# Opening order, first loads and one closing unit in a fused attention and mixer kernel on one Trainium2 core

## The chip, the cores and the metric

The kernel runs on one core of one Trainium2 chip. The core has engines that run side by side, each with its own instruction queue in order: TensorE (PE in the profile, its weight loads PEld), VectorE (DVE), ScalarE (ACT), GpSimd (POOL), and SyncE (SP), whose queue here issues the DMAs. The metric is the device time of one execution in microseconds (us), lower is better. Three runs of the kernel before gave 985.40, 985.25 and 983.98 us, median 985.25.

## What is computed

Inputs are float32: `z` (8, 3136, 64), `v` and `u` (8, 3136, 256), and the mixer's weights `U` (3136, 32), `V` (32, 3136), `w_ch1` (256, 1024) and `w_ch2` (1024, 256).

```python
scores = np.matmul(z, z.transpose(0, 2, 1)) / S        # S = 3136
attn = np.maximum(scores, 0.0) ** 2
x = u * np.matmul(attn, v)                             # attention part
h = (x.transpose(0, 2, 1) @ U) @ V                     # mixes along the sequence
u2 = x + h.transpose(0, 2, 1)
out = u2 + np.maximum(u2 @ w_ch1, 0.0) @ w_ch2
```

The score matrix of a batch is symmetric, since both factors are `z`.

## The kernel before

**Tiles and slots.** The 3136 rows of a batch are 24 tiles of 128 rows (`NF`) and a tail of 64. Four tiles make a group of 512 rows, so a batch has six full groups (`NQ`) and a small one; `NG` is 7. One (batch, group) is an item, and the main loop has one slot for each of the 56 items. In a slot TensorE does three kinds of work, cut into short units that are interleaved: the attention-by-`v` matmuls of this item (`av_stream`), the score matmuls that later items need (`todo[t]`), and the mixer matmuls of an item seven or eight slots back (`u2_unit`, `ch1_part`, `ch2_stream`). After the last slot a closing loop of `NQ + 1` stages (L1466 on) does the mixer of the last batch.

**Score pairs.** A score pair is two matmuls of 64 x 128 by 64 x 512 into the two banks of one PSUM buffer, one on the upper 64 rows of TensorE's array and one on the lower (`score_pairs`, L424; every paired matmul is recorded as `pair`'s line L182). The result goes through a scale and ReLU (`rectify`, on ScalarE at L386 or on VectorE at L382 and L393) and a square (L362 on VectorE; one early pair entirely on ScalarE, L376 and L377), and lands as bf16 in one of 20 score blocks (`take_block`). From the second batch on, and in late groups of the first, half of the score blocks come from the other half by a DMA transpose (L416 for 512 columns, L408 for pieces). For the first groups of batch 0 there is nothing to transpose from in time, and those are computed twice, so score pairs, ReLUs and squares are densest in slots 0 to 2.

**Who decides the order.** Instructions are in a manual schedule: what the Python code emits first on an engine stands first in its queue. Planner variables choose the order: `clock[0]` counts TensorE's work in units of one 256-column pair, `free_at` holds the expected times of ScalarE, VectorE and SP, `ps_free` the expected times at which the four PSUM buffers (two banks each) come free. `take_ps` takes the buffer that is expected free first, `rectify` gives work to the engine expected free first, and `hold(time, f)` puts off a DMA or a cast until the planner's clock has passed a time. These numbers set only the order; on the chip the engines wait for each other by semaphores.

**The opening.** `z` and `v` of batch 0 are loaded and cast, and `z` is turned (64 columns to partitions) by matmuls against an identity matrix, `ident`, in three turns (`z_turn`, L323: matmuls L329, copy out of PSUM L338): tiles 0 to 3, tiles 4 to 7, and an eight-tile turn of tiles 8 to 15. Two more turns (tiles 16 to 23, and the tail) follow inside slot 0, behind casts of L240. Blank matmuls of `ident` by `ident` run ahead of them: 18 at the start (L1285) and 10 ahead of the eight-tile turn (L327). They compute nothing that is used. `ident` is made by two POOL instructions. Two score pairs stand between the second and the eight-tile turn, two after it; then slot 0 starts.

**First loads.** The mixer's weights are needed only from slot 7 on. `first_loads` (L1217) says in which slot each begins: slot 1 and 2 `V` (16 DMAs of L1198, four casts into `V4_bf`), slot 3 `U` (L1156, L1157), slot 4 `w_ch1` (L1172), slot 5 `w_ch2` (L1175). All of them use SP's queue, which also carries the loads of `v` (L254), `u` (L306) and `z` (L218, L224) and the DMA transposes. The casts go to ScalarE (L202) or VectorE (L204), whichever the planner has free first, and are held back for some time after the slot's start.

**The closing loop.** For an item, `u2_unit` (L808) makes `h` in PSUM, adds `x` on VectorE (L855) and usually casts the sum and turns it by DMA (L770) for the next matmul. For the item called `direct`, the last batch's first group, the turned form is made another way (`u2T_unit`), and its `u2_unit(..., turn=False)` yields only the sum that is added to the output. In `qm.append((17, 1, False, f))` the first number is the place in the stage, counted in units of `ch2_stream`, at which `f` is emitted. Around it stand ReLUs of the first mixer layer (L944 on VectorE, L947 on ScalarE) and the output adds (L1067).

The functions that the diff touches:

Of the kernel before, what the change touches and what calls it, by code (L numbers as in the profile page):

```python
# [9 lines left out]
BF16 = mybir.dt.bfloat16  # L10
# [8 lines left out]
def kernel(  # L19
# [11 lines left out]
    nc = tc.nc  # L31

    B, S, D = u.shape
# [3 lines left out]
    P = 128  # L37
# [6 lines left out]
    GT = 4  # L44
# [10 lines left out]
    NG = len(groups)  # L55
# [6 lines left out]
    persist = ctx.enter_context(tc.tile_pool(name="persist", bufs=1))  # L62
# [3 lines left out]
    ctx.enter_context(tc.manual_schedule())  # L66

    ident = persist.tile([P, P], BF16, name="ident")
    w1_bf = persist.tile([P, ND, H], BF16, name="w1_bf")
    w2_bf = persist.tile([P, NH, D], BF16, name="w2_bf")  # L70
    U_bf = persist.tile([P, NT, R], BF16, name="U_bf")
# [5 lines left out]
    NQ = NF // GT  # L77
# [18 lines left out]
    clock = [0.0]  # L96
# [14 lines left out]
    def book(eng, ready, cost):  # L111
        free_at[eng] = max(free_at[eng], ready) + cost
        return free_at[eng]
# [5 lines left out]
    def hold(due, f):  # L119
        held.append((due, len(held), f))  # L120
# [18 lines left out]
    def pe(cost):  # L139
        clock[0] += cost  # L140
# [3 lines left out]
    ps_free = [0.0] * NPS  # L144

    def take_ps():
        k = min(range(NPS), key=lambda i: ps_free[i])
        assert ps_free[k] < float("inf")
        clock[0] = max(clock[0], ps_free[k])
        ps_free[k] = float("inf")  # L150
        for bank in range(2):
            wrote.pop((k, bank), None)
        return k, ps_pool.tile([P, 2, GW], FP32, name=f"ps{k}")
# [169 lines left out]
    def z_turn(b, t0, copy, n=2 * GT, warm=0):  # L323
        n = min(n, NT - t0)
        k, pz = take_ps()
        for _ in range(warm):
            nc.tensor.matmul(out=pz[:, 0, :P], lhsT=ident, rhs=ident, start=True, stop=True)  # L327
        for q in range(n):
            nc.tensor.matmul(  # L329
                out=pz[:, q // GT, (q % GT) * P : (q % GT + 1) * P],  # L330
                lhsT=z_bfs[b][:, t0 + q, :, :].rearrange("p c d -> p (c d)"),
                rhs=ident,
                start=(q % GT == 0),
                stop=(q % GT == GT - 1 or q == n - 1),
            )
        flat = pz.rearrange("p a c -> p (a c)")
        dst = zzTs[b].rearrange("p t c -> p (t c)")[:, t0 * P : (t0 + n) * P]
        copy(out=dst, in_=flat[:, : n * P])  # L338
        pe(8)
        ps_free[k] = book("act", clock[0] + 3, 9.5)  # L340


    def half(zzT, jj, c0, n):
# [800 lines left out]
    def jobs_of(b, g):  # L1144
        js = [J for J in range(NQ) if J >= g or made_twice(b, g, J)]
        j = [(b, g, (J, h)) for J in js for h in range(2)]
        if g % 2 == 0 and b == 0:
            j.append((b, g, "last"))
        return j
# [18 lines left out]
    def load_w(k):  # L1168
        def step(i):
            entry, raw = stage_block()  # L1170
            if k == 0:
                nc.sync.dma_start(out=raw, in_=moe_w_ch1[i * P : (i + 1) * P, :])  # L1172
                dst = w1_bf[:, i, :]
            else:
                nc.sync.dma_start(  # L1175
                    out=raw.rearrange("p (t d) -> p t d", d=D),
                    in_=moe_w_ch2.rearrange("(t p) d -> p t d", p=P)[:, i * GT : (i + 1) * GT, :],
                )
                dst = w2_bf[:, i * GT : (i + 1) * GT, :].rearrange("p t d -> p (t d)")
            queued(GT * D / 2)  # L1180

            def casts(entry=entry, raw=raw, dst=dst):
                cast(dst, raw, GT * D)
                give_block(entry)

            return [casts]

        return [lambda i=i: step(i) for i in range(2)]


    def load_V(i0):
        n = P // 4

        def step(i):
            entry, raw = stage_block()
            w = n * NF + (S - NF * P if i == 3 else 0)
            for c in range(NREP):
                nc.sync.dma_start(out=raw[c * R : (c + 1) * R, :w], in_=moe_V[:, i * n * NF : i * n * NF + w])  # L1198
                queued(w / 8)

            def casts(i=i, entry=entry, raw=raw):
                cast(
                    V4_bf[:, : NF * P].rearrange("r (t p) -> r t p", p=P)[:, :, i * n : (i + 1) * n],
                    raw[:, : n * NF].rearrange("r (p t) -> r t p", t=NF),
                    2 * n * NF,
                )
                if i == 3:
                    nc.vector.memset(V4_bf[:, S:], 0.0)
                    cast(V4_bf[:, NF * P : S], raw[:, n * NF : n * NF + S - NF * P], 100)
                give_block(entry)  # L1210

            return [casts]

        return [lambda i=i: step(i) for i in range(i0, i0 + 2)]


    first_loads = {  # L1217
        1: lambda: load_V(0),
        2: lambda: load_V(2),
        3: lambda: [load_U],  # L1220
        4: lambda: load_w(0),
        5: lambda: load_w(1),
    }


# [5 lines left out]
    on_act, on_dve, on_pool = nc.scalar.copy, nc.vector.tensor_copy, nc.gpsimd.tensor_copy  # L1231
# [49 lines left out]
    spare += [lambda i=i: cast_v(i, on_pool) for i in range(1, NQ)]  # L1281

    k, ps = take_ps()
    for _ in range(18):
        nc.tensor.matmul(out=ps[:, 0, :P], lhsT=ident, rhs=ident, start=True, stop=True)  # L1285
    ps_free[k] = 36
    cast_z(0, 0, on_dve, 0, GT)
    cast_z(0, 1, on_act, 0, GT)
# [1 line left out]
        cast_z(0, c, on_dve, GT, 2 * GT)  # L1290
    for i in range(2):
        give_block(zraw[i][2])
    clock[0] = 38
    z_turn(0, 0, on_act, GT)
    z_turn(0, GT, on_act, GT)
    clock[0] = 43
    free_at.update(dve=46, act=47)
    jobs0 = jobs_of(0, 0)
    score_burst(jobs0[:1])
    score_burst(jobs0[1:2])  # L1300
    clock[0] = 56
    z_turn(0, 2 * GT, on_act, warm=10)
    score_burst(jobs0[2:3])
    score_burst(jobs0[3:4])
    clock[0] = 72

    todo = {t: [] for t in range(n_items)}
    for b in range(B):
        for g in range(NQ):
            t = b * NG + g - 1  # L1310
            new = jobs_of(b, g)
            if g == 0 and b > 0:
                x, y = (5, 10) if b == 1 else (5, 11)
                todo[t - 2] += new[:x]
                todo[t - 1] += new[x:y]
                todo[t] += new[y:12] if b == 1 else new[y:]
                todo[t + 1] += new[12:] if b == 1 else []
            elif b == 0 and g == 0:
                todo[0] += new[4:]
            elif b == 0 and g and g % 2 == 0:  # L1320
                todo[t] += new[:-1]
                todo[t + 1] += new[-1:]
            else:
                todo[t] += new

    for t, most in ((0, 15), (1, 16), (2, 13)):
        todo[t + 1] = todo[t][most:] + todo[t + 1]
        todo[t] = todo[t][:most]

    direct = (B - 1, 0)  # L1330
# [4 lines left out]
    for t in range(n_items):  # L1335
# [6 lines left out]
        g_now = t % NG  # L1342
        b_next = t // NG + 1
# [6 lines left out]
            xTs[direct] = take_block()[1][:, : GT // 2, :].rearrange("p a (q d c) -> p (a q) d c", d=ND, c=P)  # L1350
            x_turn(*direct, xTs[direct])
        for i, f in enumerate(casts_next):
            hold(clock[0] + (90 if g_now == NQ and b_next > 1 else 15 if t >= NQ else 45) + 12 * i, f)
        casts_next = []
        spare += spare_next
        spare_next.clear()
# [26 lines left out]
        qc, qs, qm = [], [], []  # L1383
# [13 lines left out]
        if av and full:  # L1397
# [5 lines left out]
            n = len(mine) - 3  # L1403
            qs += [(9 + 74 * i / n, 1, False, lambda: scores(1)) for i in range(n)]
        elif av:
# [5 lines left out]
            k = min(2, len(mine) // 3)  # L1411
            n = len(mine) - 3 * k
            at = [1 + 80 * i / n for i in range(n)]
            if t == 0:
                at, k = [14, 30, 44, 50, 64, 68, 78, 84, 92], 0
# [46 lines left out]
    def small_parts(item, places):  # L1462
        box = {}
        return [(x, 1 - way, False, lambda way=way: ch1_small(*item, way, box)) for way, x in enumerate(places)]

    for k in range(NQ + 1):  # L1466
        fin = (B - 1, k - 1) if k else (B - 2, NQ - 1)
        mix = (B - 1, k) if k < NQ else None
        light = ch2_halves(*fin) if k == NQ else ch2_stream(*fin, {}).units
        first, qm = parts(mix, {}) if mix else [], []  # L1470
        if k == 0:
            qc = small_parts((B - 2, NQ), (13, 19)) + queue((16, 18, 20, 21, 24, 26, 28, 30), first)
            qm.append((3, 0, False, lambda: u2T_unit(*direct)))
            qm.append((9, 1, False, lambda: u2_unit(B - 1, 1)))
            qm.append((17, 1, False, lambda: u2_unit(*direct, turn=False)))
            qm.append((25, 1, False, lambda: u2_unit(B - 1, 2)))
        else:
            last = k == NQ - 1
            qc = queue((1, 2, 5, 6, 10, 11, 14, 16) if last else (1, 4, 8, 12, 16, 20, 24, 28), first)
            if k + 2 <= NQ:  # L1480
                qm.append((2, 1, False, lambda: u2_unit(B - 1, k + 2)))
            if last:
                qc += small_parts((B - 1, NQ), (18, 23))
            if k == 1 or k == NQ:
                qm.append((9, 1, False, lambda b=B - 2 if k == 1 else B - 1: ch2_small(b, NQ)))
        emit(light, [qc, qm])
# [30 lines left out]
```

## Time and profile before

The profiled execution took 985.75 us; its span in the trace is 984.0 us.

| what | number |
|---|---|
| median of three runs | 985.25 us |
| profiled execution / its span | 985.75 / 984.0 us |
| TensorE busy | 974.5 us (99%) |
| VectorE busy | 630.0 us (64%) |
| ScalarE busy | 484.3 us (49%) |
| POOL busy | 16.5 us (2%) |
| matmuls | 16165 |
| symmetric turns and other DMA transposes (blk from blk) | 156, 5.2 us each from issue to landing |
| weights `w_ch1`, `w_ch2` | 4 DMAs of 512 KB, 7.6 us each |

In a timeline line the numbers are start and length in us, then engine, line, operation, tiles (out, then in), the shape and the count of instructions taken together; square brackets hold the engine's idle time before the line and what ended it. The chain is followed back from the last instruction, and shows at each step what released it.

### The profile page before, as it was taken

Reading aid. Unit: us, or ns where it says so; the run is one execution under the profiler, and the core shown is the slowest. Engines: PE = TensorE matmul, PEld = TensorE weight load, DVE = VectorE, ACT = ScalarE, POOL = GpSimd, SP = SyncE. Lnnn points to the kernel's source line nnn. Section 1 sums busy time; section 2 is a strip of 40 time slices with the busy share of each in tenths; the row PEclk is TensorE's granted clock in tenths of the full one; section 3 lists DMA queues with packets and bytes.
Section 4 is the critical chain, followed back from the end, with each engine's and each line's share of the span. In section 5 each row is a group of like instructions: output and inputs, shape, how many; then the busy total and the mean of one; then the engine's idle time right before and its main releaser. Section 6 shows DMA issues by size and latency. Waiting matters only on the chain.

```text
span 984.0 us, 35373 instructions
## 1 busy us (share of the span) xinstructions
PE 974.5 (99%) x16165; PEld 778.2 (79%) x16165; DVE 630.0 (64%) x811; ACT 484.3 (49%) x560; POOL 16.5 (2%) x25
## 2 busy tenths in 40 slices
PE   9999999999999999999999999999999999999998
PEld 6788777877778777787777877788777887778766
DVE  7877855668556685567755667556775567653363
ACT  7887732456324463355533555334653345531353
POOL 4100000000000000000000000000000000000000
PEclk9999999999999999999999999999999999999999
DMA  9999999979997799987999779998799978975143
GB/s 266 201 237 205 219 191 187 220 152 186 203 207 158 174 184 188 213 167 180 182 203 207 146 178 191 212 198 147 173 211 202 194 148 165 177 136 103 46 113 99
DMA packets 372405, 176.37 MB, mean 179 GB/s; under 512 B 347296, under 2 KB 350624, under 8 KB 372256
## 3 DMA queue, kind: packets, MB, share of 16 engines
q1 hardware_dynamic: 372256, 174.12, 86.4%
q8 instruction: 126, 2.06, 0.9%
q14 instruction: 23, 0.19, 0.1%
HBM read 62.56 MB, written 25.69 MB: 90 GB/s over the span
## 4 chain that ended last, share of the span: by engine, by line
PE 94%; DVE 2%; ACT 2%; DMA 1%; SPq 0%; POOL 0%; issue 0%; DVEq 0%; POOLq 0%
PE ps L182 91%; DVE blk L362 1%; PE ps L701 1%; ACT blk L386 1%; PE ps L782 1%; DMA u2T<-x_bf 1%; DMA blk<-in_moe_V_dram 0%; PE ps L1081 0%; DVE blk L382 0%; PE ps L1285 0%; ACT blk L947 0%; PE ps L329 0%; POOL v_bf L1246 0%; PE ps L327 0%; SPq L1198 0%
## 5 line engine op out<-in xcount | busy, mean ns | idle before, releaser
L182 PEld LDWEIGHTS <-blk 64*128 64x128 bf16 x12288 | 613.8, 94 | 153.3 <-POOLq L172 9.5
L182 PE MATMUL ps<-v_bf,blk 64*128 64x256 bf16 x9216 | 611.7, 269 | 0.3
L386 ACT ACTIVATE blk<-ps 128x1024 bf16<-128x1024 f32 (+1 forms) x331 | 312.1, 971 | 343.8 <-PE ps L182 341.7
L362 DVE TENSOR_TENSOR blk<-blk 128x1024 bf16<-128x1024 bf16 x351 | 222.7, 659 | 46.6 <-ACT blk L386 45.9
L182 PE MATMUL ps<-u2T,w_bf 64*128 64x512 bf16 (+1 forms) x1792 | 227.7, 349 | 0.3 <-DMA u2T<-x_bf 0.2
L182 PE MATMUL ps<-w_bf,blk 64*128 64x256 bf16 x3072 | 192.4, 269 | 0.2 <-ACT blk L947 0.2
L944 DVE TENSOR_SCALAR blk<-ps 128x1024 bf16<-128x1024 f32 x106 | 129.7, 1224 | 93.3 <-PE ps L182 92.3
L947 ACT ACTIVATE blk<-ps 128x1024 bf16<-128x1024 f32 x86 | 87.3, 1022 | 117.8 <-PE ps L182 117.5
L182 PE MATMUL ps<-zzT 64*128 64x512 bf16 (+2 forms) x902 | 130.8, 328 | 2.2 <-ACT blk L386 1.5
L182 PEld LDWEIGHTS <-w_bf 64*128 64x128 bf16 x1792 | 84.4, 94 | 27.4 <-POOLq L172 5.0
L734 DVE TENSOR_TENSOR x_bf<-ps,u_sb 128x1024 bf16<-128x1024 f32 x48 | 58.7, 1222 | 72.8 <-PE ps L182 72.8
L855 DVE TENSOR_TENSOR out_sb<-ps,x_bf 128x1024 f32<-128x1024 f32 x42 | 51.4, 1223 | 59.1 <-PE ps L182 59.1
L1067 DVE TENSOR_TENSOR out_sb<-ps,out_sb 128x1024 f32<-128x1024 f32 x42 | 51.4, 1224 | 18.6 <-PE ps L182 18.3
L182 PEld LDWEIGHTS <-zzT 64*128 64x128 bf16 x902 | 41.7, 94 | 8.6 <-issue 3.9
L382 DVE TENSOR_SCALAR blk<-ps 128x1024 bf16<-128x1024 f32 (+1 forms) x17 | 19.6, 1159 | 7.1 <-PE ps L182 7.1
L182 PE MATMUL ps<-t_sb,V_bf 64*128 64x256 bf16 x200 | 20.6, 269 | 0.0
L202 ACT CAST v_bf<-stage 128x1024 bf16<-128x1024 f32 x18 | 18.7, 1042 | 0.0
L182 PE MATMUL ps<-v_bf,last_sb 64*128 64x256 bf16 x192 | 18.5, 269 | 0.2 <-POOLq L172 0.2
L204 DVE CAST v_bf<-stage 128x1024 bf16<-128x1024 f32 (+1 forms) x30 | 18.1, 603 | 0.0
L204 DVE CAST x_bf<-out_sb 128x1024 bf16<-128x1024 f32 x21 | 14.5, 688 | 0.3
L202 ACT CAST x_bf<-out_sb 128x1024 bf16<-128x1024 f32 x14 | 14.5, 1037 | 0.0
L362 DVE TENSOR_TENSOR attn_small<-attn_small 128x1600 bf16<-128x1600 bf16 x8 | 7.9, 990 | 9.0 <-ACT attn_small L591 9.0
(80 smaller groups left out, 241.1 us busy)
## 6 DMA issues: line engine op xcount, KB each, us to landing
u_sb<-in_u_dram SPq DMA_DIRECT2D x48, 512.0 KB, 5.0
stage<-in_v_dram SPq DMA_DIRECT2D x42, 512.0 KB, 6.1
out_dram<-out_sb SPq DMA_DIRECT2D x42, 512.0 KB, 3.1
stage<-in_z_dram SPq DMA_DIRECT2D x7, 512.0 KB, 5.9
blk<-in_v_dram SPq DMA_DIRECT2D x5, 512.0 KB, 6.3
out_dram<-blk SPq DMA_DIRECT2D x5, 512.0 KB, 2.6
blk<-blk SPq DMA_TRANSPOSE x156, 5.2
blk<-in_moe_w_ch_dram SPq DMA_DIRECT2D x4, 512.0 KB, 7.6
```

The lines of the kernel that those rows point to most:

```text
L182: ins = nc.tensor.matmul(**args)
L202: nc.scalar.copy(out=out, in_=in_)
L204: nc.vector.tensor_copy(out=out, in_=in_)
L362: nc.vector.tensor_tensor(out=a, in0=a, in1=a, op=ALU.mult)
L382: nc.vector.tensor_scalar(out=dst, in0=src, scalar1=scale, scalar2=0.0, op0=ALU.mult, op1=ALU.max)
L386: nc.scalar.activation(out=dst, in_=src, func=AF.Relu, scale=scale)
L701: nc.tensor.matmul(out=ps[c * hp : c * hp + rows, h, :D], lhsT=smalls[b][h * hp : (h + 1) * hp, place_of(jt), :], rhs=v_bfs[b][h * hp : (h ...
L734: nc.vector.tensor_tensor(out=xs[b, g][:rows, :n, :], in0=four(box["ps"])[:rows, :n, :], in1=u_sbs[b, g][:rows, :n, :], op=ALU.mult,)
L855: nc.vector.tensor_tensor(out=o[:rows, :n, :], in0=four(ps)[:rows, :n, :], in1=x, op=ALU.add)
L944: nc.vector.tensor_single_scalar(out=r, in_=ps[:, :, :gw], scalar=0.0, op=ALU.max)
L947: nc.scalar.activation(out=r, in_=ps[:, :, :gw], func=AF.Relu)
L1067: nc.vector.tensor_tensor(out=o, in0=acc, in1=o, op=ALU.add)
```

## The change

Five things change.

1. A tile `blank` of zeros, filled by a VectorE memset, takes the place of `ident` in the blank matmuls. There are 21 at the start (18 before) and 5 ahead of the second four-tile turn (none before), and none ahead of the eight-tile turn (10 before): 26 in all, 28 before.
2. All four of the first score pairs stand ahead of the eight-tile turn. The planner's clock is set to 32, 58 and 68 at the marked places (38, 56 and 72 before), and `z_turn` books TensorE and ScalarE in proportion to its tiles.
3. Slot 0's score list starts with one pair of the second group, which that group's own list then leaves out. At most 14, 15 and 14 pairs stay in slots 0, 1 and 2 (15, 16 and 13 before).
4. The first loads begin with `U` in slot 2; `V` follows in slots 3 and 4, `w_ch1` in 5 and `w_ch2` in 6. Casts in slot 7 are held for 60 planner units (15 before).
5. In the closing loop the direct item's `u2_unit` moves from stage 0, place 17, to stage 1, place 13, and the unit that was at place 25 of stage 0 is at place 17.

```diff
     ident = persist.tile([P, P], BF16, name="ident")
+    blank = persist.tile([P, P], BF16, name="blank")
+    nc.vector.memset(blank, 0.0)
...
         for _ in range(warm):
-            nc.tensor.matmul(out=pz[:, 0, :P], lhsT=ident, rhs=ident, start=True, stop=True)
+            nc.tensor.matmul(out=pz[:, 0, :P], lhsT=blank, rhs=blank, start=True, stop=True)
...
-        pe(8)
-        ps_free[k] = book("act", clock[0] + 3, 9.5)
+        pe(n)
+        ps_free[k] = book("act", clock[0] + 3, 9.5 * n / (2 * GT))
...
     first_loads = {
-        1: lambda: load_V(0),
-        2: lambda: load_V(2),
-        3: lambda: [load_U],
-        4: lambda: load_w(0),
-        5: lambda: load_w(1),
+        2: lambda: [load_U],
+        3: lambda: load_V(0),
+        4: lambda: load_V(2),
+        5: lambda: load_w(0),
+        6: lambda: load_w(1),
     }
...
-    for _ in range(18):
-        nc.tensor.matmul(out=ps[:, 0, :P], lhsT=ident, rhs=ident, start=True, stop=True)
+    for _ in range(21):
+        nc.tensor.matmul(out=ps[:, 0, :P], lhsT=blank, rhs=blank, start=True, stop=True)
...
-    clock[0] = 38
+    clock[0] = 32
     z_turn(0, 0, on_act, GT)
-    z_turn(0, GT, on_act, GT)
+    z_turn(0, GT, on_act, GT, warm=5)
     clock[0] = 43
     free_at.update(dve=46, act=47)
     jobs0 = jobs_of(0, 0)
     score_burst(jobs0[:1])
     score_burst(jobs0[1:2])
-    clock[0] = 56
-    z_turn(0, 2 * GT, on_act, warm=10)
     score_burst(jobs0[2:3])
     score_burst(jobs0[3:4])
-    clock[0] = 72
+    clock[0] = 58
+    z_turn(0, 2 * GT, on_act)
+    clock[0] = 68
...
             elif b == 0 and g == 0:
-                todo[0] += new[4:]
+                todo[0] += jobs_of(0, 1)[:1] + new[4:]
+            elif b == 0 and g == 1:
+                todo[t] += new[1:]
...
-    for t, most in ((0, 15), (1, 16), (2, 13)):
+    for t, most in ((0, 14), (1, 15), (2, 14)):
...
-            hold(clock[0] + (90 if g_now == NQ and b_next > 1 else 15 if t >= NQ else 45) + 12 * i, f)
+            hold(clock[0] + (90 if g_now == NQ and b_next > 1 else 60 if t == NG else 15 if t >= NQ else 45) + 12 * i, f)
...
             qm.append((9, 1, False, lambda: u2_unit(B - 1, 1)))
-            qm.append((17, 1, False, lambda: u2_unit(*direct, turn=False)))
-            qm.append((25, 1, False, lambda: u2_unit(B - 1, 2)))
+            qm.append((17, 1, False, lambda: u2_unit(B - 1, 2)))
...
+            if k == 1:
+                qm.append((13, 1, False, lambda: u2_unit(*direct, turn=False)))
```

## The prediction

> **What bounds the kernel now.** I read the windows by stage first, then TensorE's timeline in the stages where it is not full, then the chain of waits there. The rows of the windows give stretch, length, and the busy time of PE, PEld, DVE, ACT and POOL.
>
> ```profile
> 0.00:10.00 10.00, 7.85 (x60) 5.43 (x62) 3.63 (x6) 6.41 (x8) 3.10 (x10) 1.00 0.79 259
> 10.00:30.00 20.00, 19.42 (x281) 13.13 (x277) 17.34 (x25) 16.90 (x19) 8.89 (x10) 1.00 1.02 265
> 30.00:60.00 30.00, 28.06 (x448) 23.47 (x446) 28.23 (x37) 26.02 (x26) 4.55 (x5) 1.00 0.93 194
> 60.00:112.00 52.00, 51.82 (x953) 44.70 (x951) 39.40 (x64) 39.40 (x49) 0.00 (x0) 1.00 1.00 225
> 112.00:928.00 816.00, 816.00 (x13645) 654.13 (x13645) 511.37 (x649) 370.09 (x432) 0.00 (x0) 1.00 0.89 178
> 928.00:984.00 56.00, 51.34 (x796) 37.40 (x796) 30.05 (x34) 25.53 (x29) 0.00 (x0) 0.99 0.37 99
> ```
>
> From 112 to 928 us TensorE is busy 816.00 of 816.00 us, and the change leaves its order there alone. Only four matmuls go away in the whole program (two blanks with their weight loads make four rows), so all that can be won lies in the holes before 112 and in the closing 56 us. From 30 to 60 us VectorE is busy 28.23 of 30 and ScalarE 26.02: while every score pair has still to be computed twice, these two set the pace.
>
> TensorE's timeline (start, length, line, tiles, count, idle before it):
>
> ```profile
> 1.36 2.10 PE L1285 MATMUL ps<-ident 128*128 128x128 bf16 x18 [1.36 <-POOL ident masks.py:199]
> 6.41 1.23 PE L327 MATMUL ps<-ident 128*128 128x128 bf16 x10 [0.69 <-ACT blk L376]
> 7.43 1.06 PE L329 MATMUL ps<-ident,z_bf 128*128 128x128 bf16 x8
> 14.16 0.62 PE L329 MATMUL ps<-ident,z_bf 128*128 128x128 bf16 x8
> 39.75 0.39 PE L182 MATMUL ps<-zzT 64*128 64x512 bf16 x2 [0.52 <-ACT blk L386]
> 45.31 0.39 PE L182 MATMUL ps<-zzT 64*128 64x512 bf16 x2 [0.48 <-DVE x_bf L734]
> 55.02 0.39 PE L182 MATMUL ps<-zzT 64*128 64x512 bf16 x2 [0.94 <-ACT blk L386]
> ```
>
> Three score bursts in slots 1 and 2 wait for a PSUM buffer that ScalarE or VectorE has not emptied. The longest stands behind two V casts, as ScalarE's rows show:
>
> ```profile
> 49.05 2.08 ACT L202 CAST V_bf<-blk 128x768 bf16<-128x768 f32 x1
> ...
> 51.03 1.03 ACT L386 ACTIVATE blk<-ps 128x1024 bf16<-128x1024 f32 x1
> ...
> 51.95 2.09 ACT L202 CAST V_bf<-blk 128x768 bf16<-128x768 f32 x1
> ...
> 53.93 2.86 ACT L386 ACTIVATE blk<-ps 128x1024 bf16<-128x1024 f32 x3
> ```
>
> The chain near the end has two plain ReLU waits:
>
> ```profile
> 937.38 1.03 ACT blk L947
> ...
> 938.45 2.90 PE ps L182 x38
> ...
> 941.38 1.03 ACT blk L947
> ```
>
> **How the holes are counted.** For every matmul I took the time from its start to the next start and subtracted the pace of its kind (0.109 us for a pair of 256 columns at full speed). What is over is a stall, and it is larger than the printed idle time because the tail of the last matmul hides part of it: 0.70, 0.66 and 1.11 us at 39.75, 45.31 and 55.02.
>
> **The first turns (0 to 14.2 us).** (a) The blanks now need a VectorE memset in place of the identity. VectorE's other memsets in this trace take 0.085 to 0.165 us, against 0.20 and 0.29 us on POOL, so the blanks may start near 0.9 instead of 1.36. This wins nothing: the first transposes at 3.40 wait for the z cast, which ends at 3.35. Twenty-one blanks at 0.107 to 0.117 us end by 3.4 too. (b) Five blanks ahead of the second turn cost 5 x 0.107 = 0.54 us on TensorE, of which 0.36 pushes the turn, since it stood idle or waiting there for the rest. (c) The four score pairs then run from about 4.75 to 6.42 instead of 4.69 to 9.25. The third turn follows when ReLU frees its buffer at about 6.65, where it was at 7.43, and the ten blanks of L327 (1.23 us, filling a wait) go. The first 16 attention-by-v matmuls could end at 9.0 instead of 10.65.
> (d) That lead of 1.65 us meets VectorE's queue. It works in order: scale and ReLU of one pair (1.23), three squares (0.65 each, the third behind ScalarE's ReLU that ends near 9.7), the added second-group pair (1.23), its square, and then the two z casts (11.54, 1.58 us together in the trace) on which the next turn at 14.16 waits. My replay puts their end at 13.9. So 1.65 shrinks to 0.25. Ends: 0.3 lost if the added pair's 1.2 us hits the casts fully; 0.6 won. I take +0.25, since it is the replay's own value.
>
> [...]
>
> **Rest of slot 0 (14.2 to 27).** Stalls here sum to about 1.6 us (0.29 at 21.32, 0.37 at 26.14 and 0.30 at 27.85 the largest). Those at 21 to 26 follow POOL's v casts, whose two-cast groups take 1.64 to 1.93 us and stay. One pair fewer (14 instead of 15) takes away 0.97 us of ScalarE and 0.65 of VectorE. Ends 0 and 0.7; I take +0.3, the one at 27.85.
>
> **Slots 1 and 2 (27 to 57).** Stalls sum to 0.16 + 0.15 + 0.14 + 0.70 + 0.66 + 1.11 = 2.92 us. Moved out: V's casts, two shown above and one like them at 2.09 on ScalarE, some 4.2 us of them before 57, and two V issue groups of SP's queue (26.72 for 4.64 us, 46.43 for 4.77), behind which symmetric transposes stood (L416 at 34.70 and 52.73). Moved in: U's load and cast, 0.56 and 0.17. The pairs done by the ends of slots 0, 1 and 2 (the four first ones and the limits added up: 4 + 15, + 16, + 13, against 4 + 14, + 15, + 14) go from 19, 35, 48 to 18, 33, 47, which again relieves ScalarE by 0.97 and VectorE by 0.65 each. That is about 2.5 us per engine against holes of 2.92. The 1.11 goes wholly, since its cause is named. I take +2.2, nearer to the relief; the ends are 0.8 (only the named one, with a new small hole of 0.3) and 2.9 (all).
>
> **Where the moved work lands (57 to 112).** TensorE is busy 51.82 of 52.00 us, VectorE and ScalarE 39.40 each, so there is room: four V casts on VectorE at 1.10 (row at 64.56) and w's casts at 1.04. What is late next: w2's first half now stands behind two transposes of SP's queue (88.04 to 98.39 holds three of them in the trace), its second half behind the tail's transpose (98.39) and one of z's loads. Weights take 7.6 us from issue to landing; I place the first half's issue near 92.5 and its cast, which ScalarE meets in order, near 99.5, while its data land near 100. While it waits, the ReLUs behind it wait, and TensorE for their PSUM. V's sixteen issues, 9.4 us of SP time, now stand ahead of the transposes of slots 3 and 4. I take -0.3; ends 0 and -1.5.
>
> **Closing part (928 to 984).** The x + h unit of the direct group goes one stage later and the other is pulled from place 25 to 17. Each holds a 1.23 us add and ScalarE's or VectorE's cast of 1.04 or 0.69. The stalls at 938.45 (0.41) and 942.45 (0.31) stand where two adds, a cast and ReLUs crowd. I take the first as gone and a third of the second: +0.5; ends -0.3 (u2 needed sooner than its transpose is done) and +0.72.
>
> **Sum.** 0.25 + 0.3 + 2.2 - 0.3 + 0.5 = 2.95 us. The profiled execution took 985.75 us (span 984.0, and 1.75 around it), 0.5 above the median of 985.25. So 982.8 against its own time, 982.3 against the median. All best ends give 4.9 (980.35); all worst, -0.3 + 0 + 0.8 - 1.5 - 0.3 = -1.3 (986.55).
>
> **Rivals.** *The holes move on.* Slots 1 and 2 still contain back-to-back double bursts (four 512-column matmuls at 49.55, for instance), with VectorE 94% busy; work taken from ScalarE would not help where VectorE is the late one, as it is at 45.31. For it: 45.31's releaser is VectorE. Against: VectorE is relieved of pairs too. Then only the start, 55.02 with its new hole and the end remain: 0.25 + 0.8 + 0.5 - 0.3 = 1.25, so 984.0.
> *Slower: ScalarE blocks on w2.* If w2's first half is issued one transpose later than I place it, ScalarE stands still for the difference. TensorE runs on for about 1 us on the buffers in hand (a cast of 2.09 left a stall of 1.11 at 55.02). From a lateness of 2.95 + 1.0, about 4 us, the gain is used up, and at 7.6, a full load behind, 6.6 are lost: 985.25 - 2.95 + 6.6 = 988.9. For it: DMA share 1.00 in that window, so nothing lands early. Against: in the trace of before w2 is issued at 85.70 and cast from 100.77 on, and my placing of the queue has the lateness at 0 to 2.
> *The early lead survives.* If VectorE does its z casts before the added pair, the next turn comes at up to 1.65 less the 0.25 earlier and all best ends are possible: 980.4. The trace of before has the casts right behind the first squares, but the written order has the added pair ahead of them.
>
> **How the numbers follow.** About 0.2%, 2.0 us, can be told from no change here. Forecast, 982.3 with 980.9 to 983.3 of its own: 0.48. Lead survives: 0.08. Holes move on, 983.3 to 987.2: 0.30. ScalarE blocks: 0.14, nearly all slower. That gives 0.56 faster, 0.30 within and 0.14 slower. The range leaves out 0.05 below and the blocked case above: 980.2 to 986.6.
>
> **What would show it.** Right: the turn now at 14.16 starts near 13.9; no printed wait over 0.5 us on TensorE from 27 to 57; V's casts on VectorE only, after 70; TensorE full from 60 to 112; the wait at 938.45 gone. Wrong: a wait of TensorE on ScalarE's ReLU near 50 as before (the holes moved on); an idle time of ScalarE before a w cast that ends on a DMA near 99 (blocking); a new idle time before the direct group's matmuls in the closing part, which would turn that term's sign; or a turn after 14.5, which says the added pair costs more than it saves.

## The result and the profile after

The changed kernel takes 982.23 us (median of 11 runs, 981.84 to 984.80) against 985.14 us for the kernel before (11 runs beside it). The ratio is 0.9978, 95% interval 0.9971 to 0.9986: 0.2% faster, with the forecast at 982.3 and the range at 980.2 to 986.6. Measured again beside the last experiments it was 982.65 against 984.08, ratio 0.9981 (0.9972 to 0.9990). The profiled execution took 982.0 us with a span of 980.2, so the two profiles differ by 3.75 us in time and 3.8 in span. That is more than the medians differ by, and the reason is the main thing that the experiments found.

Windows by stage of the changed kernel (stretch, length, busy time of PE, PEld, DVE, ACT and POOL):

```profile
10.00:30.00 20.00, 17.97 (x267) 12.18 (x263) 15.57 (x24) 16.40 (x19) 8.18 (x11) 1.00 1.01 260
30.00:60.00 30.00, 30.00 (x498) 24.24 (x494) 27.47 (x39) 25.99 (x28) 4.17 (x5) 1.00 0.92 187
60.00:112.00 52.00, 52.00 (x949) 43.20 (x947) 41.97 (x66) 37.46 (x48) 0.00 (x0) 1.00 1.06 227
```

From 30 to 60 us TensorE is now busy 30.00 of 30 (28.06 before), with VectorE and ScalarE as busy as they were. Slot 0, in the first row, is not better: 17.97 of 20 (19.42 before). TensorE's timeline shows why:

```profile
3.73 0.74 PE L329 MATMUL ps<-blank 128*128 128x128 bf16 x5
...
6.50 0.61 PE L331 MATMUL ps<-ident,z_bf 128*128 128x128 bf16 x8 [0.32 <-ACT blk L378]
7.59 0.61 PE L184 MATMUL ps<-v_bf,blk 64*128 64x256 bf16 x8 [0.49 <-ACT blk L379]
8.69 0.61 PE L184 MATMUL ps<-v_bf,blk 64*128 64x256 bf16 x8 [0.49 <-POOL v_bf L1248]
13.09 0.62 PE L331 MATMUL ps<-ident,z_bf 128*128 128x128 bf16 x8 [0.57 <-DVE z_bf L242]
18.15 0.28 PE L184 MATMUL ps<-v_bf,blk 64*128 64x256 bf16 x2 [0.59 <-DVE blk L364]
28.02 0.28 PE L184 MATMUL ps<-v_bf,blk 64*128 64x256 bf16 x2 [0.39 <-DVE blk L364]
```

The eight transposes of the third turn take 0.61 us, where they took 1.06, so TensorE is already at full pace at 6.5 us (before: only after 10.3). Attention by `v` starts at 7.59 instead of 9.25, the turn of tiles 16 to 23 at 13.09 instead of 14.16. Then VectorE's squares hold TensorE at 18.15, and most of the lead is gone.

ScalarE's row around 50 us holds ReLUs alone, where two V casts of 2.09 us stood between them:

```profile
46.37 7.48 ACT L388 ACTIVATE blk<-ps 128x1024 bf16<-128x1024 f32 x8
```

One milestone for each stage, VectorE's output of a group (L734, L736 after), gives the account, in us earlier than before:

| up to | earlier | of this stage | forecast |
|---|---|---|---|
| first group's output (slot 0) | 0.42 | 0.42, of which 0.22 is one pair fewer | 0.25 + 0.3 |
| fourth group's (slots 1 to 3) | 2.93 | 2.51 | 2.2 |
| eighth group's (slots 4 to 7, with the wait at 111.8) | 3.28 | 0.35 | -0.3 |
| end of the span | 3.8 | 0.53 | 0.5 |

(At the fifth group the lead reads 1.04 and at the third 4.62, since the pairs are dealt to the slots differently there.) A second profile of the changed kernel (experiment 11, span 981.0 us) gives 0.19, 2.51, -0.18 and 0.52 for the four stages, so the first and the third row differ from one execution to the next.

Of the signs that the prediction named, four came: no printed wait over 0.5 us on TensorE from 27 to 57, V's casts on VectorE alone (the first at 74.63), TensorE full from 60 to 112, and the wait ahead of 938.45 gone. The turn came at 13.09 instead of near 13.9. In the closing part the chain of the changed kernel runs through one stretch of matmuls, where the chain before went over two ReLUs:

```profile
925.58 12.82 PE ps L184 x198
938.39 0.03 issue
938.42 0.83 PE ps L184 x8
```

### The profile page after: what moved, and what is told of

Read it like the earlier page. It is cut to its first block, busy times and chain, and to the rows that moved or that the text cites. A ratio compares the mean times of both kernels' runs of the same rounds, so it can differ in the third digit from the quotient of the medians.

```text
span 980.2 us, 35372 instructions
## 1 busy us (share of the span) xinstructions
PE 971.5 (99%) x16163; PEld 774.0 (79%) x16163; DVE 627.5 (64%) x811; ACT 481.5 (49%) x561; POOL 15.9 (2%) x25
## 4 chain that ended last, share of the span: by engine, by line
PE 97%; DMA 1%; SPq 1%; DVE 0%; POOL 0%; issue 0%; DVEq 0%; ACT 0%; POOLq 0%
PE ps L184 94%; PE ps L703 1%; DMA blk<-in_v_dram 1%; PE ps L784 1%; PE ps L1083 0%; DMA u_sb<-in_u_dram 0%; SPq L220 0%; POOL v_bf L1248 0%; SPq L1261 0%; SPq L226 0%; DVE x_bf L736 0%; SPq L256 0%; DVE blk L724 0%; DVE blk L364 0%; DVE blk L1055 0%
## 5 line engine op out<-in xcount | busy, mean ns | idle before, releaser
L364 DVE TENSOR_TENSOR blk<-blk 128x1024 bf16<-128x1024 bf16 (+1 forms) x350 | 221.2, 656 | 50.0 <-ACT blk L388 49.3
L736 DVE TENSOR_TENSOR x_bf<-ps,u_sb 128x1024 bf16<-128x1024 f32 x48 | 58.7, 1222 | 72.6 <-PE ps L184 72.6
L384 DVE TENSOR_SCALAR blk<-ps 128x1024 bf16<-128x1024 f32 (+1 forms) x14 | 16.1, 1147 | 5.3 <-PE ps L184 5.3
L204 ACT CAST v_bf<-stage 128x1024 bf16<-128x1024 f32 (+1 forms) x17 | 17.0, 1003 | 0.0
L1069 DVE TENSOR_TENSOR blk<-ps,blk 128x1024 f32<-128x1024 f32 x5 | 6.1, 1225 | 11.9 <-PE ps L184 11.8
```

The source lines that it names most:

```text
L204: nc.scalar.copy(out=out, in_=in_)
L364: nc.vector.tensor_tensor(out=a, in0=a, in1=a, op=ALU.mult)
L384: nc.vector.tensor_scalar(out=dst, in0=src, scalar1=scale, scalar2=0.0, op0=ALU.mult, op1=ALU.max)
L736: nc.vector.tensor_tensor(out=xs[b, g][:rows, :n, :], in0=four(box["ps"])[:rows, :n, :], in1=u_sbs[b, g][:rows, :n, :], op=ALU.mult,)
L1069: nc.vector.tensor_tensor(out=o, in0=acc, in1=o, op=ALU.add)
```

## Experiments

The measured times have a spread of about a microsecond, so what a part does is read mainly from the milestones and the waits of each trace.

**1. The closing loop alone.**

```diff
-            qm.append((17, 1, False, lambda: u2_unit(*direct, turn=False)))
-            qm.append((25, 1, False, lambda: u2_unit(B - 1, 2)))
+            qm.append((17, 1, False, lambda: u2_unit(B - 1, 2)))
...
+            if k == 1:
+                qm.append((13, 1, False, lambda: u2_unit(*direct, turn=False)))
```

> The kernel before with the closing loop's reordering alone. Theory (the parts add up, each in its own stage): TensorE is as before up to 928 us; the stall of 0.41 us ahead of 938.45 goes and that of 0.31 at 942.45 shrinks to 0.19, as in the changed kernel, so 0.5 us less, about 984.6 against 985.1. Rival (the closing gain needs the earlier start): no difference, 985.1.

Median 983.72 us, ratio 0.9995 (0.9986 to 1.0004). In the trace the stall of 0.41 us ahead of 938.45 is gone and that of 0.31 is 0.19, as expected: 0.53 us. But the span was 981.8, 2.2 us shorter. The rest came from an opening whose instructions are those of the kernel before. TensorE's timeline of this run:

```profile
6.42 0.72 PE L327 MATMUL ps<-ident 128*128 128x128 bf16 x10 [0.69 <-ACT blk L376]
6.97 0.61 PE L329 MATMUL ps<-ident,z_bf 128*128 128x128 bf16 x8
7.51 0.61 PE L182 MATMUL ps<-zzT 64*128 64x512 bf16 x4
7.96 0.60 PE L182 MATMUL ps<-v_bf,blk 64*128 64x256 bf16 x8
...
12.70 0.62 PE L329 MATMUL ps<-ident,z_bf 128*128 128x128 bf16 x8
```

The same ten blanks that took 1.23 us take 0.72 here, and the turn of tiles 16 to 23 starts at 12.70 instead of 14.16; the first group's output comes 1.31 us earlier. So one kernel has two openings. The times show it: of the 99 runs of the kernel before that were made beside the experiments, 49 took 983.77 to 984.76 us and 50 took 985.12 to 986.68, with none between. The eleven runs of this experiment fall apart in the same way, six at 983.37 to 983.72 and five at 984.60 to 985.41. I call them early-clock and late-clock executions; the profile on which the prediction rests was a late-clock one.

Each trace also holds a record of the clock granted to TensorE. It begins when full clock is granted: at 10.32 us in the profile of before and at 5.66 in this run. (Nothing is recorded ahead of that moment, so the clock column of the windows rows reads 1.00 from the start and hides the slower pace.) Both traces have the wait of 0.69 us on ScalarE ahead of the ten blanks, ending at 6.42 in this run, behind the grant, and at 6.41 in the profile of before, ahead of it. That this wait held the clock back in the one and not in the other was my guess; what set the moment of the grant is not shown.

**2. The later first loads alone.**

```diff
-        1: lambda: load_V(0),
-        2: lambda: load_V(2),
-        3: lambda: [load_U],
-        4: lambda: load_w(0),
-        5: lambda: load_w(1),
+        2: lambda: [load_U],
+        3: lambda: load_V(0),
+        4: lambda: load_V(2),
+        5: lambda: load_w(0),
+        6: lambda: load_w(1),
```

(with the hold of 60 in slot 7)

> The kernel before with the later first loads (and the later hold of casts in slot 7) alone. Theory 1 (V's casts on ScalarE are what made slots 1 and 2 stall): the stall of 1.11 us at 55.02 goes, and with it one of the smaller ones, and the wait of 0.35 at 111.8 goes: 1.1 to 2.2 us less, 983 to 984. Theory 2 (the number of score pairs made by the end of each slot is what counts, and the casts fill ScalarE's idle time): less than 0.5 us, 984.7 or more, with waits of TensorE on ScalarE's ReLU of over 0.4 us left between 38 and 57.

Median 984.86, ratio 0.9992 (0.9983 to 1.0000). The stall at 55.02 is gone, those at 39.65 and 45.21 (0.70 and 0.66) are as before, and the sixth group's output is 1.20 us earlier than in the late-clock profile of before. Then 1.0 of it is lost in one place:

```profile
111.58 0.61 PE L182 MATMUL ps<-u2T,w_bf 64*128 64x512 bf16 x4 [1.15 <-DMA u2T<-x_bf]
```

That DMA transpose landed 6.83 us after its issue, against 5.86 before. The runs fall into two groups here too, five at 982.66 to 983.15 us and six at 984.86 to 985.86, and the profiled one (full clock from 10.91) is of the later. Theory 1 holds for the one stall, and only for it.

**3. The opening and the score lists together, and 4. the score lists alone.** The third run takes the blank tile, the order of the first pairs, the second-group pair and the limits; the fourth only the last two:

```diff
-                todo[0] += new[4:]
+                todo[0] += jobs_of(0, 1)[:1] + new[4:]
+            elif b == 0 and g == 1:
+                todo[t] += new[1:]
...
-    for t, most in ((0, 15), (1, 16), (2, 13)):
+    for t, most in ((0, 14), (1, 15), (2, 14)):
```

> The kernel before with the opening alone: blank tile, four first pairs ahead of the eight-tile turn, the second-group pair and the limits 14, 15, 14; first loads and closing loop as before. Theory 1 (V's casts): the stall behind the casts near 50 to 55 stays or moves, and the start gives about 0.2 net in slot 0 and 0.7 to 1.4 from the stalls at 39.75 and 45.31: 983.5 to 984.3. Theory 2 (pair counts): nearly all of the 2.65 us of slots 1 and 2 comes with this part: 982.3 to 982.9.

> The kernel before with the second-group pair in slot 0 and the limits 14, 15, 14 alone; blanks, first pairs, loads and closing loop as before. Theory 2 (pair counts): 1.5 us or more less, 983.6 or lower. Theory 1 (V's casts, and the early start): 0 to 0.7 us less, 984.4 to 985.1, with the stall behind V's casts still there.

The third took 983.75 (0.9990, 0.9982 to 0.9999), the fourth 984.64 (1.0001, 0.9987 to 1.0015), with runs from 982.67 to 990.43. Both trace the same between 27 and 57 us: the stalls at 39.75 and 45.31 are gone, and of the 1.11 behind V's casts 0.50 is left:

```profile
53.03 0.39 PE L182 MATMUL ps<-zzT 64*128 64x512 bf16 x2 [0.33 <-ACT blk L386]
```

Neither theory was whole. The score lists take 2.0 of the 2.5 us of slots 1 to 3 (the fourth run's fourth group is 1.44 earlier, after a first group 0.57 later), and they seem to act partly through V's casts. With other pair counts the planner, which gives each cast to the engine that it expects free first, put V's casts on VectorE, where one takes 1.10 us instead of 2.09. VectorE's rows of the fourth run:

```profile
48.13 1.10 DVE L204 CAST V_bf<-blk 128x768 bf16<-128x768 f32 x1
...
49.74 1.11 DVE L204 CAST V_bf<-blk 128x768 bf16<-128x768 f32 x1
```

ScalarE meanwhile runs nine ReLUs without a break (8.38 us from 47.36). The sixth group's output is 1.44 us earlier than before, both with a late clock, although the first group's was 0.57 later, with new waits on VectorE's squares in slot 0 (0.76 us at 19.14). In the third run it is 1.74 earlier, with an early clock (6.31). How much of the smaller stall is due to the engine of V's casts, and how much to the pair counts, was not separated.

**5. Opening alone (blank tile and order of the first pairs).**

```diff
-    z_turn(0, 2 * GT, on_act, warm=10)
     score_burst(jobs0[2:3])
     score_burst(jobs0[3:4])
-    clock[0] = 72
+    clock[0] = 58
+    z_turn(0, 2 * GT, on_act)
+    clock[0] = 68
```

(with blanks, `warm=5` and planner costs as in the changed kernel)

> The kernel before with the blank tile and the four first pairs ahead of the eight-tile turn (with its planner clocks) alone; score lists, limits, loads and closing loop as before. [...] The stalls of slots 1 and 2 (0.70, 0.66 and 1.11) stay. Rival (the opening gains only its own 0.25 us): two groups 1.3 us apart as before, median near 985.

Median 985.20, ratio 1.0001 (0.9992 to 1.0010). I expected one group of runs, at or below 983.9, and a matmul pace that doubles before 8 us. Half of that came true: ten of eleven runs lie between 984.93 and 985.31, one group, and full clock is granted at 5.87 us. But the group lies at the late-clock time of before. In the trace a new wait takes the lead:

```profile
10.48 0.39 PE L184 MATMUL ps<-zzT 64*128 64x512 bf16 x2 [1.38 <-ACT zzT L340]
```

Its stall is 1.56 us; from 4 to 14.2 us all stalls sum to 4.58, against 3.06 in experiment 1. Slot 0's first own pair needs the eight-tile turn, whose copy (L340) ScalarE does only after two ReLUs, from 9.42 to 10.43. The stalls of slots 1 and 2 (0.70, 0.66, 1.13) are untouched.

**6. Score lists and later loads, old opening.**

> The kernel before with the second-group pair, the limits and the later first loads; opening and closing loop as before. If the pair limits take the stalls at 39.75 and 45.31 and the V casts what is left of 55.02, TensorE has no stall above 0.3 us between 30 and 90, as in the changed kernel, and the sixth group's VectorE output comes 1.9 us earlier than before; at 111 TensorE waits for the transposed u2 by 0.3 to 1.3 us. Since the opening is that of before, the runs still form two groups: about 982.9 and 984.2. Rival (the early opening is needed for slots 1 and 2 too): one stall of 0.5 us or more stays between 30 and 57.

Median 983.76, ratio 0.9994 (0.9981 to 1.0007). Between 30 and 112 us the trace has no stall above 0.1 us. The sixth group's output is 1.79 us earlier than before, both with a late clock (9.34 here). From the first group's output to the fourth's, loads alone gain 1.11, lists alone 2.01, and both together 2.51, as much as the changed kernel. So the two parts overlap, and the new opening is not needed for slots 1 to 3: the rival falls. The wait for the transposed u2 that I expected was not there. The runs spread from 982.34 to 987.72, with three near 982.4, four near 983.7 and four from 985.23 on, so beside two groups there is a tail that I cannot explain.

**7. The changed kernel with one blank instead of 21 and none ahead of the second turn.**

```diff
-    for _ in range(21):
+    for _ in range(1):
...
-    z_turn(0, GT, on_act, GT, warm=5)
+    z_turn(0, GT, on_act, GT)
```

> The changed kernel with one blank matmul instead of 21 at the start and none ahead of the second turn. [...] Rival (blanks do nothing, the first z cast and VectorE's queue set the opening): 982.2, no difference from the changed kernel.

I expected a later clock, and 0.5 to 1.3 us lost by it in the opening: 982.7 to 983.5. Median 984.50 (981.91 to 987.12), ratio 0.9999 (0.9987 to 1.0010). In the profiled execution full clock was granted at 6.71 us, and its opening was even 0.15 us ahead of the changed kernel's; it then waited 2.50 us for the transposed u2, which landed 8.18 us after its issue. So the median is some 2 us above the changed kernel's (982.23 and 982.65, not measured beside it), but the trace does not show the expected cause: the clock did turn 1.4 to 1.6 us later than in the two profiles of the changed kernel, and the opening lost nothing by it. The granted clock of the four longest runs (985.88 to 987.12) is 0.997 to 0.998, that of the other seven 0.999 or 1.000; none of the four was traced, and 0.997 also stands beside runs of 983.00 and 983.26 in experiment 10, so this settles nothing. What the blanks are worth in this order is left open.

**8. The kernel before with one blank at the start.**

```diff
-    for _ in range(18):
+    for _ in range(1):
```

> The kernel before with one blank matmul at the start instead of 18, and the ten ahead of the eight-tile turn kept. [...]

I expected the early group to vanish, with all runs at 985 to 986.5. Median 986.27, all eleven runs between 985.38 and 988.51, beside a kernel before of which 22 of 33 runs lay below 984.8 (median 984.08); ratio 1.0021 (1.0012 to 1.0030). The early group is gone. The trace, in which the ten blanks take 1.22 us and the eight transposes 1.06, against 0.72 and 0.61 in experiment 1:

```profile
3.33 1.20 PE L329 MATMUL ps<-ident,z_bf 128*128 128x128 bf16 x8 [1.69 <-ACT z_bf L240]
4.62 1.03 PE L182 MATMUL ps<-zzT 64*128 64x512 bf16 x4
6.34 1.22 PE L327 MATMUL ps<-ident 128*128 128x128 bf16 x10 [0.69 <-ACT blk L376]
7.36 1.06 PE L329 MATMUL ps<-ident,z_bf 128*128 128x128 bf16 x8
```

Full clock is granted at 10.96 us, and with one blank instead of 18 none of the eleven runs lies in the early group, as expected; whether the blanks act on the clock, and how, is not shown. A late clock does not account for all of the time, since the median lies about 1 us above the late-clock runs of before (985.12 to 985.55 beside it), and a stall of 0.44 us at 946.94 explains part of one profile only.

**9. VectorE's z casts earlier (place 18 to 4 in slot 0 of the changed kernel).**

> The changed kernel with VectorE's two z casts for the turn of tiles 16 to 23 at place 4 of slot 0 instead of 18; in VectorE's queue they then stand behind the first square, ahead of three squares and the second-group pair's scale and ReLU. If VectorE's casts hold that turn (0.73 us at 13.09) and nothing else is near, 0.5 to 0.7 us less than the changed kernel. If z's third piece lands only near 8.5, the squares that attention by v waits for near 8.7 and 10.3 come 1.2 us later: the stall moves there, and the time is 982.2 to 983.

Median 982.83, ratio 0.9980 (0.9971 to 0.9989), against 982.23 and 982.65 of the changed kernel at other times: no gain. The wait moves to the squares that attention by `v` needs:

```profile
11.64 1.21 PE L184 MATMUL ps<-v_bf,blk 64*128 64x256 bf16 x16 [1.09 <-DVE blk L364]
```

The first group's output is 0.62 us later than in the changed kernel, so in slot 0 TensorE waits for VectorE with either order of its queue.

**10. The changed kernel without the second-group pair at the head of slot 0.**

> The changed kernel without the second-group pair at the head of slot 0 (it goes back into its own group's list; limits, opening, loads, closing loop as changed). Theory: that pair needs only the first two turns, and fills TensorE while ScalarE, behind two ReLUs, copies out the eight-tile turn; without it the next pair waits for that copy, as in the kernel with the opening alone: a wait of 1.2 to 1.5 us on ScalarE's zzT copy near 10.4, and 0.4 to 1.3 us lost: 982.6 to 983.5. Rival (the pair is only one pair more): no such wait, 982.2 or less.

Median 983.00 (981.63 to 985.95), ratio 0.9983 (0.9974 to 0.9992), beside 982.65 for the changed kernel. The wait on ScalarE's copy was there, smaller than expected (0.86 us idle at 10.17), but the two waits on VectorE's squares at 16.7 and 18.15 (0.17 and 0.76 us) were gone, and the first group's output came at 25.88, against 26.15 and 26.38 in the two profiles of the changed kernel. The profile also has a wait of 0.85 us at 346.60 for which no cause shows, so its span, 981.0, says little. The pair moves a wait; a gain from it is not shown. Nor is it needed for slots 1 and 2, where this trace has no stall but the one of 0.57 at 27.77.

**11. The changed kernel again, and 12. with the second weights loaded one slot earlier.**

```diff
-        5: lambda: load_w(0),
-        6: lambda: load_w(1),
+        5: lambda: load_w(0) + load_w(1),
```

> The changed kernel again, beside the next three on one chip. If its opening has no slow group, at least nine of eleven runs lie within 1.2 us of the fastest, near 982; the rest, if any, are late at 111 us. Otherwise two groups 1.3 us apart show.

> The changed kernel with the second weights loaded in slot 5 with the first ones instead of slot 6; in SP's queue each half then stands one transpose earlier. Theory (the wait for the transposed u2 near 109 to 111, 0 in the changed kernel's profile but 1.3 and 2.7 us in two other kernels with the late loads, comes from loads issued just ahead of it on busy DMA engines): w2's second half is out some 5 us before that transpose, so no run shows a late tail; median as the changed kernel or up to 0.4 less. Rival: earlier loads delay the symmetric transposes before them, and slots 6 and 7 wait: 0.3 us or more lost.

The changed kernel: nine of eleven runs between 981.51 and 982.84, two at 983.71 and 984.30. Its profile has a wait of 0.37 us on the transposed u2 that the first profile of the same kernel lacks. With the earlier weights: 982.88 (981.87 to 984.01), ratio 0.9987 (0.9978 to 0.9996), no such wait in the profile, but two runs as late as without it. So neither theory is borne out, and the few later runs of the changed kernel stay unexplained.

## Why the prediction was right, and where it was not

**The total was right in part by luck.** The sum, 2.95 us, was made against a late-clock execution, and seven of the eleven runs of before that stood beside the result were late-clock ones too. Taken from the two groups of before (near 983.9 and 985.3) to the median of the changed kernel's 22 runs, 982.6, the gain is about 1.3 us against the one and 2.7 against the other. The traces show the same difference: the changed kernel's profile leads by 3.8 us on the late-clock profile of before, but by about 2.2 on an early-clock one (at the sixth group's output 2.92 less the 1.30 that experiment 1 shows, so 1.62, and 0.53 in the closing loop); that both leads are larger than the medians' is mostly because the profiled execution, 982.0, was one of the quicker of its kernel, and that of before, 985.75, one of the slower. The median moved by 2.9 where most executions of before had a late clock, and by 1.4 where 22 of 33 had an early one. That half of the executions would differ by 1.3 us was in no term and no rival.

**The first turns: +0.25, measured +1.07 at the turn of tiles 16 to 23** (0.83 in the second profile of the changed kernel). The step that was wrong reads, of VectorE's two z casts: "My replay puts their end at 13.9." They ended at 13.04 (13.27 in the second profile). They began at 11.87 instead of the replay's 12.3, and they took 1.17 us where the row of before had 1.58. One row of ScalarE and two of VectorE after the change, and the casts' row before it:

```profile
7.44 1.92 ACT L388 ACTIVATE blk<-ps 128x1024 bf16<-128x1024 f32 x2
...
9.39 0.69 DVE L364 TENSOR_TENSOR blk<-blk 128x1024 bf16<-128x1024 bf16 x1 [0.22 <-ACT blk L388]
...
11.87 1.17 DVE L242 CAST z_bf<-blk 128x512 bf16<-128x512 f32 x2
...
11.54 1.58 DVE L240 CAST z_bf<-blk 128x512 bf16<-128x512 f32 x2
```

The square that the prediction put behind a ReLU ending near 9.7 waits for one that ends at 9.36; ScalarE has worked almost without a pause since its second copy at 4.93. That is most of the earlier start. As for their length, each z cast takes 0.41 to 0.44 us or 0.82 to 0.84 (here one of each, before two long ones). All 17 long ones in the fourteen traces have a POOL cast beside them, and the five with none are short; but two short ones have a POOL cast beside them almost throughout, so the cause is not settled. That the earlier clock brought the casts forward is not shown, and experiment 12 speaks against it: there full clock came at 7.02, later than in the changed kernel's profiles (5.10 and 5.34), the casts ended at 12.74 and the turn came at 12.85.

What the opening did change is the clock, which is in no term of the sum. In the seven traces that have it in whole full clock was granted between 3.87 and 7.02 us; in the five with the opening of before four times between 9.34 and 10.91 and once at 5.66. The runs of experiment 5 form one group. What this is worth in time is not shown. That one group lies at the late-clock time. At the end of slot 0 the changed kernel's lead is 0.42, against 1.31 in experiment 1 with the old opening and an early clock. The three quickest runs of experiment 6, also with the old opening, would come to about 981.9 with the closing part's 0.53 taken off, and its four near 983.7 to about 983.2 (an estimate); the changed kernel's median, 982.6, lies between. So the new opening seems to replace two openings by one, and not to beat the better of them.

**Rest of slot 0: +0.3, measured a loss of 0.65** between the turn and the first group's output, although one pair fewer gives 0.22 there. The term took the stall at 27.85 as gone. It came back as 0.57 at 28.02, just behind that output, and VectorE's squares made new ones of 0.17 and 0.76 at 16.7 and 18.15. Over the whole of slot 0 the forecast was 0.55 and the measurement 0.42 (0.19 in the second profile), so two errors of opposite sign nearly cancelled: that, too, was luck.

**Slots 1 and 2: +2.2, measured 2.5.** Size and place were right: all three stalls went. The mechanism was right for 55.02 and incomplete for the rest. I charged 4.2 us of V's casts to the loads and little to the limits. The later loads alone take the stall at 55.02 (experiment 2); the score lists alone take those at 39.75 and 45.31 and move V's casts to VectorE as well (experiment 4). Both together give the 2.51 with the old opening (experiment 6).

**57 to 112: -0.3, measured +0.35, and a matter of chance.** The wait for the transposed u2 was 0.35 us in before's profile, 0 in one of the changed kernel, 0.53 (0.37 of it idle) in the other, so the second profile has a loss of 0.18 in this stage. In the fourteen traces that DMA landed 4.0 to 8.2 us after its issue, and TensorE waited for it by more than 0.1 us in exactly the six in which it took 5.7 us or more. Three of these six have the loads of before (the profile of before, experiments 3 and 4), so the later loads are not needed to make it late. ScalarE's block on w2's cast, the slower rival, was seen once, 0.43 us in experiment 7:

```profile
100.71 1.05 ACT L204 CAST w_bf<-blk 128x1024 bf16<-128x1024 f32 x1 [0.43 <-DMA blk<-in_moe_w_ch_dram]
```

TensorE did not wait for ScalarE behind it, and the wait that followed at 111.07 was on the transposed u2.

**Closing part: +0.5, measured 0.53:** each of the seven traces with the new order has the stall of 0.41 gone and that of 0.31 at 0.19. By experiment 1 it is independent of the rest.

**The rivals.** The holes did not move on in slots 1 and 2; they did in slot 0. The early lead survived further than I forecast, by another way than the one that I named: experiment 9 made that way and it gave nothing.

## What to carry to other kernels

Before a gain of a few tenths of a per cent is counted from one profile, look whether the runs fall into groups, and which group the profile belongs to; here the base itself moved by 1.3 us, half of the forecast. The same opening instructions can run at two paces: here full clock came at 5.66 us in one trace and at 10.32 in another, and the times lie in two groups 1.3 us apart. That the wait of 0.7 us at 5.7 us decides between them was not shown. An earlier clock wins only what the other engines allow: with the new opening alone it came at 5.87, a wait of 1.38 us on ScalarE's copy followed, and the median stayed at 985.20. In a schedule written by a planner, a changed limit also moves work between engines, so read the engine of each cast again after the change.

## What was not expected of the hardware

- Full clock was granted to TensorE at 10.32 us in one execution and at 5.66 in another with the same opening instructions (ten blanks in 1.23 and 0.72 us), and the kernel's times split into 983.8 to 984.8 and 985.1 to 986.7 us. With one blank instead of 18 the lower group vanished.
- The same cast of V (128 x 768) took 2.09 us on ScalarE and 1.10 on VectorE.
- VectorE's cast of z (128 x 512) took 0.41 to 0.44 or 0.82 to 0.84 us, the longer time only with a cast on POOL beside it; whether that is the cause was not tested.
- The DMA transpose of u2 issued between 102 and 106 us landed 4.0 to 8.2 us after its issue. One and the same kernel gave 5.5 and 6.0, and two kernels with the same loads 4.2 and 8.2; what sets it was not found.
